# One chunk's transpose moved from TensorE to a DMA that ScalarE gives out

## The chip, the cores and the metric

One core of a Trainium2 chip runs the whole program. The metric is the device time of one launch in microseconds (us). Beside it stands one profiled execution, whose span reaches from its first to its last instruction. Engines: PE is TensorE's matmul side and PEld its weight load, DVE is VectorE, ACT is ScalarE, POOL is GpSimd, SP is SyncE. SP does no arithmetic here; its instructions give out DMAs. ACT can give out DMAs too, on a queue of its own; in the profile such instructions are listed as SPq and ACTq.

## The reference

A retention layer feeds a gated feed-forward layer. Inputs are float32: q, k, v of shape (8 batches, 8 heads, 576 positions, 64) and three weight matrices.

```python
scores = (1 / sqrt(64)) * q @ k.T                     # per batch and head
gamma  = 1 - 2.0 ** (-5 - head)
ret    = (scores * where(i >= j, gamma ** (i - j), 0)) @ v
x      = ret.transpose(0, 2, 1, 3).reshape(4608, 512)
out    = (sigmoid(x @ w_gate) * (x @ w_val)) @ w_out  # w_gate, w_val 512x1536; w_out 1536x512
```

## The kernel before

The 4608 tokens are worked off in chunks of 128 positions. The first 768 tokens go as three pairs of chunks; every later chunk is a *step* `s` (0 to 29), a batch and a chunk of it from the table `STEPS`. The powers of gamma are multiplied into q and k when they are cast to bf16 (`cast_qk`, line 420, into the tile `qk_s`; k's part on POOL, q's part on DVE for steps 0 and 1 and on POOL after that). The mask then needs only zeros and ones, and what earlier chunks contribute comes from a running state, a 64 by 64 matrix for each head.

TensorE's matmul contracts over partitions, so q and k must stand with the head dimension on the partitions. The tile `T_s` holds them turned. There are two ways to it:

- `cross(s)` (line 446) gives out one DMA crossbar transpose on SP's queue, from `qk_s` to `T_s`. It is called by `casts_to` (line 853) between the casts of k and q and the cast of v, for every step not in `TURNED`.
- `turn_step(s)` (line 624), for the steps in `TURNED = (0, 1, 7)`: eight 128x128 transposes on PE into two PSUM banks, which ACT (the first half of `T_s`) and DVE (the second half) copy out.

Tokens run through the feed-forward layer in blocks: tokens 0 to 511 first, then blocks of 256 (512 to 767, called `w = 0`, and 768 to 1023), then blocks of 512. Every engine works its own list of instructions strictly in the order in which the code recorded it; the framework adds the waits. The code around the change runs so:

1. `op_first` (line 1542) makes the output product of the first 512 tokens: 12 weight slices `fc` into four PSUM tiles. The first `FIRST_OP_CUTS = 20` products with `fc > 0` are written as two halves of 256 columns.
2. Between its last slices stands `turn_step(0)`; after it `casts_to(1)` casts step 1.
3. The block `w = 0` runs its hidden units (`h_units`, line 877): for six pairs of slices a gate tile `h_g` (8 matmuls, then a sigmoid on ACT into `gv`) and a value tile `h_v` (8 matmuls, then a multiplication on DVE into `gv`). Both come from the same three PSUM banks, tag `ffn`, dealt round: `h_v_4` takes the bank that `h_g_2` had, and so waits until ACT has read `h_g_2`.
4. Into these units the string `SUMS_AT` deals small jobs. An entry such as `0.6:t01p` means: in block 0, before unit 6, job `t` (`turn_step`) for step 1. `0.0:c03p` is `casts_to(3)`, which casts steps 2 and 3 and gives out their transposes and the loads of step 4 on SP.
5. After unit 10 of `w = 0` the first two steps are used: `slot_of_two` (line 741) makes their scores (`row`, line 686) from `T_0` and `T_1`, and the products of k and v for the state.

DMAs are counted on eight semaphores, DMAHW0 to DMAHW7, that the framework deals round in the order in which DMAs are recorded, whatever queue gives them out; each DMA waits at least for the one that had its semaphore before.

Of the kernel before, what the change touches and what calls it, by code (L numbers as in the profile page):

```python
# [16 lines left out]
def kernel(  # L17
# [19 lines left out]
    nc = tc.nc  # L37
# [109 lines left out]
    def half(x):  # L147
        return slice(x * 64, x * 64 + 64)
# [169 lines left out]
    def wo_sums(i, part, parts, eng=nc.vector):  # L318

        fp = slice(part * (NFC // 2) // parts, (part + 1) * (NFC // 2) // parts)  # L320
        b11, b12, b21, b22 = (wo_sb[:, r::2, c:c + DM // 2][:, fp] for r in range(2) for c in (0, DM // 2))
        t1, t2, t4 = (wt_sb[:, j, fp] for j in range(3))
        to, a, b = ((t1, b12, b11), (t2, b22, t1), (b12, b22, b12), (t4, b21, t2))[i]
        eng.tensor_tensor(out=to, in0=a, in1=b, op=ALU.subtract)
# [34 lines left out]
    def w_sums(kind, i, u, eng):  # L359

        a11, a12, a21, a22 = w_quarters(kind, u)
        s1, s2, s4 = (wt3_sb[kind][j][u] for j in range(3))
        to, a, b, op = ((s1, a21, a22, ALU.add), (s2, s1, a11, ALU.subtract), (seventh(kind, u), a11, a21, ALU.subtract),
                        (s4, a12, s2, ALU.subtract))[i]
        eng.tensor_tensor(out=to, in0=a, in1=b, op=op)
# [54 lines left out]
    def cast_qk(s, i, eng):  # L420
        c = STEPS[s][1]
        if i == 1:
            natural_qk[s] = nat_pool.tile([P, 2, M, P], BF16, tag="qk", name=f"qk_{s}")
        to = natural_qk[s][:, i].rearrange("p m (y d) -> p y m d", y=2)
        if i == 1 and s >= SCALED_V:
            (on_pool if s in K_ON_POOL else on_act)(out=to, in_=by_halves(loaded[s][0]))
            return
        tab = (qtab, ktab)[i][:, c, :].rearrange("p (y m) -> p y m", y=2).unsqueeze(3).to_broadcast([P, 2, M, D])
        eng.tensor_tensor(out=to, in0=by_halves(loaded[s][1 - i]), in1=tab, op=ALU.mult)  # L429
# [8 lines left out]
    def cast_v(s, eng):  # L438
        natural["v", s] = nat_pool.tile([P, H, D], BF16, tag="v", name=f"v_{s}", bufs=6)
        if s >= SCALED_V:  # L440
            tab = ktab[:, STEPS[s][1], :].unsqueeze(2).to_broadcast([P, H, D])
            nc.gpsimd.tensor_tensor(out=natural["v", s], in0=loaded[s][2], in1=tab, op=ALU.mult)  # L442
        else:
            eng(out=natural["v", s], in_=loaded[s][2])

    def cross(s):
        t = att_pool.tile([P, 2, M, P], BF16, tag="T", name=f"T_{s}", bufs=6)
        nc.sync.dma_start_transpose(out=t.rearrange("p j m t -> p (j m) t"),
                                    in_=natural_qk[s].rearrange("p j m d -> p (j m d)"))
        turned[s] = t  # L450

# [167 lines left out]
            cols = slice(t0, t0 + P)  # L619
            eng(out=x_out(slice(i * k, (i + 1) * k), cols), in_=x_in(ps[:, at_m:at_m + k], cols))  # L620

    TURNED = (0, 1, 7)

    def turn_step(s):

        t = att_pool.tile([P, 2, M, P], BF16, tag="T", name=f"T_{s}", bufs=6)
        for i, ((pool, tag), eng) in enumerate(zip(VALS, (on_act, on_dve))):
            ps = pool.tile([P, M, P], BF16, tag=tag, name=f"turn_{s}_{i}")
            for m in range(M):
                nc.tensor.matmul(ps[:, m, :], lhsT=natural_qk[s][:, i, m, :], rhs=ident, is_transpose=True,  # L630
                                 start=(m == 0), stop=(m == M - 1))
            eng(out=t[:, i], in_=ps)
        turned[s] = t
# [6 lines left out]
    def new_state(key, dt=BF16):  # L640
        b, c, j = key
        if dt == BF16 and c == LAST - 1 and j == NJ - 1:
            return nat_pool.tile([P, M, D], dt, tag="sf", name=f"sf_{b}_{c}_{j}", bufs=5)
        tag, bufs = ("s32", 3) if dt == FP32 else ("sb", 4)
        if (tag, b, c) not in both_steps:
            both_steps[tag, b, c] = nat_pool.tile([P, NJ, M, D], dt, tag=tag, name=f"{tag}_{b}_{c}", bufs=bufs)
        return both_steps[tag, b, c][:, j]
# [142 lines left out]
    def after_two(vals, news, i, late, first, closes):  # L790

        if i == 0 and not news:
            for s in vals:
                inter(s, [(1,), (0,)])
        if i < NJ:
            if len(vals) == 2 and at_col[vals[1]] == at_col[vals[0]] + P:
                leave_two(vals, i)
            else:
                for s in vals:
                    nc.scalar.copy(out=x_out(ALL, cols_of(s, i)), in_=x_in(val_ps[s][i], cols_of(s, i)))  # L800
        if i == NJ:
            for s in vals:
                if dealt(cols_of(s, 0)):
                    x_sums(at_col[s], X_LATE if late and closes else X_FIRST)
        if late and news and i == (NJ if closes else NJ - 1):
            casts_to(min(done["cast"], news[-1] + LEAD_CAST + 1) if first and not closes else news[-1] + LEAD_CAST + 1)
        for n, s in enumerate(news):
            b, c = STEPS[s]
            if c == LAST:
                continue  # L810
            if i == n:
                add_state(s, 0)
                add_state(s, 1)
                if s < 2 * len(PAIRS_AT) and s == max(x for x in news if STEPS[x][1] < LAST):
                    ffn_psum.free_last(ffn_psum.held.pop())
            if i == n + 1:
                keep_both(b, c, [j for j in range(NJ) if totals.pop((s, j), None) is not None], on_act)
# [16 lines left out]
    def first_batch_state():  # L834

        whole = new_state((0, LAST - 1, NJ - 1))
        for hh in range(2):
            for y in range(2):
                (nc.vector.tensor_copy if hh == y else nc.sync.dma_start)(
                    out=whole[half(y), hh::2, :], in_=sbd[3][half(hh), 2 * y:2 * y + 2, half(hh)])  # L840
        state[0, LAST - 1, NJ - 1] = whole
# [6 lines left out]
    def loads_to(s):  # L848
        while done["ld"] <= min(NS - 1, s):
            load(done["ld"])  # L850
            done["ld"] += 1

    def casts_to(s):
        while done["cast"] <= min(NS - 1, s):
            x = done["cast"]
            loads_to(x + (AHEAD[x] if x < len(AHEAD) else 2))
            cast_qk(x, 1, nc.gpsimd)
            cast_qk(x, 0, nc.vector if x < 2 else nc.gpsimd)
            if x not in TURNED:
                cross(x)  # L860
            cast_v(x, on_dve if x == 0 else on_act if x in V_ON_ACT else on_pool)
            done["cast"] += 1
# [6 lines left out]
    def next_two(vals, news, late, first, closes):  # L869
        slot_of_two(vals, news)  # L870
        if news and not late:
            casts_to(news[-1] + 2)
        for i in range(3):
            pending.append(lambda i=i: after_two(vals, news, i, late, first, closes))
# [661 lines left out]
    for i in (0, 1, 3):  # L1536
        w_sums("g", i, 1, nc.vector)

    FIRST_OP_CUTS = 20
    op_cut = []  # L1540

    def op_first(fcs, nbs, opps):
        for fc in fcs:
            for nb in nbs:
                parts = 2 if fc and len(op_cut) < FIRST_OP_CUTS else 1
                op_cut.extend([fc] * (parts - 1))
# [27 lines left out]
    keep_state((1, 0, 1), st_tiles[1], on_act)  # L1574
    op_first((5, 6, 7, 8, 9), range(3), opps)
    casts_to(0)
    third_intra([PV, QK[0]])
    pair_st(2, 1)
# [15 lines left out]
    store(opps[3], 3 * P, on_act)  # L1594
    casts_to(1)

    SUMS_AT = ("0.0:c03p 0.1:f00p 0.3:g00p 0.3:w10v 0.3:w11v 0.6:t01p 0.7:o10p 0.8:c02v "
# [4 lines left out]
    sums_at = {}  # L1602
    for x in SUMS_AT:
        at, x = x.split(":")
        u, i, eng = int(x[1]), int(x[2]), nc.gpsimd if x[3] == "p" else nc.vector
        sums_at.setdefault(tuple(int(y) for y in at.split(".")), []).append(
            lambda k=x[0], u=u, i=i, eng=eng: wo_sums(i, u, 3, eng) if k == "o" else
            casts_to(10 * u + i) if k == "c" else turn_step(i) if k == "t" else first_batch_state() if k == "f" else
            w_sums(k, i, u, eng))
    PAIRS_AT = ((0, 10), (0, 11), (1, 10), (1, 0))  # L1610
    paired = 0
# [80 lines left out]
```

## Time and profile before

| what | value |
|---|---|
| median of 3 runs | 304.57 us (303.11 to 306.47) |
| profiled execution, its own time | 303.89 us |
| profiled execution, span | 302.2 us |
| PE busy | 295.6 us, 98% of the span |
| DVE, POOL, ACT busy | 230.4, 225.8, 204.9 us |
| mean granted TensorE clock | 0.999 |
| crossbar transposes | 27, all on SP's queue |

A line of the timeline gives start, length, engine, line of the kernel, operation, output and input, and how many instructions it merges; in square brackets stands the idle time just before and what ended it. The profiled execution is 1.69 us longer than its span, for what lies before the first and after the last instruction.

### The profile page before, as it was taken

How to read it: one execution, taken by the hardware profiler on the slowest of the kernel's cores; microseconds unless marked ns; L12 is line 12 of the kernel's file. 1: busy time of each engine (PE TensorE's matmuls, PEld its weight loads, DVE VectorE, ACT ScalarE, POOL GpSimd, SP SyncE). 2: the span in 40 equal slices, each digit the busy share in tenths (PEclk: the TensorE clock that was granted, in tenths of full speed). 3: DMA queues.
4: the chain of work that ended last, by engine and by line, in shares of the span. 5: the costliest groups of instructions: out<-in, count | busy, mean ns of one | idle time of the engine just before them, and what ended most of it. 6: DMA issues, size and time to landing. Idle time of an engine off the chain costs nothing.

```text
span 302.2 us, 10696 instructions
## 1 busy us (share of the span) xinstructions
PE 295.6 (98%) x4437; PEld 250.0 (83%) x4437; DVE 230.4 (76%) x439; ACT 204.9 (68%) x414; POOL 225.8 (75%) x253
## 2 busy tenths in 40 slices
PE   7999999999999999999999999999999999999994
PEld 3677876978868888888888888888888888888883
DVE  5967895796986998789748974896489848935893
ACT  6755565335369657985798589857985698559830
POOL 5775854846669888978997898789978946860780
PEclk9999999999999999999999999999999999999999
DMA  7999999979998989999749967976694165004013
GB/s 205 336 370 379 322 334 229 210 160 202 213 175 184 257 173 196 219 201 262 141 108 199 259 143 155 218 185 143 124 204 132 37 123 193 4 2 139 3 36 104
DMA packets 146464, 54.99 MB, mean 182 GB/s; under 512 B 124400, under 2 KB 139760, under 8 KB 146416
## 3 DMA queue, kind: packets, MB, share of 16 engines
q1 hardware_dynamic: 145328, 53.59, 73.6%
q8 instruction: 34, 0.56, 0.8%
q10 hardware_dynamic: 1088, 0.72, 0.8%
q14 instruction: 14, 0.11, 0.1%
HBM read 37.75 MB, written 9.44 MB: 156 GB/s over the span
## 4 chain that ended last, share of the span: by engine, by line
PE 92%; DVE 2%; DMA 2%; issue 1%; ACT 1%; POOL 0%; SPq 0%; DVEq 0%
PE gatea L1046 12%; PE wa L1046 11%; PE qa L1173 11%; PE qe L1173 9%; PE gatee L1046 6%; PE we L1046 5%; PE op L1549 4%; PE h_v L886 3%; PE h_g L886 3%; PE gateg L1046 3%; PE wg L1046 3%; PE hv L1374 3%; PE op L1306 3%; PE val L718 2%; PE qa L1249 2%; PE hg L1374 2%
## 5 line engine op out<-in xcount | busy, mean ns | idle before, releaser
L1046 PEld LDWEIGHTS <-wg_sb 128*128 128x128 bf16 x348 | 34.1, 98 | 4.1
L1073 POOL TENSOR_TENSOR gv<-gv,wu 128x512 bf16<-128x512 bf16 x20 | 23.5, 1174 | 15.5 <-DVE wu L1085 15.4
L1173 PEld LDWEIGHTS <-gsum 128*128 128x128 bf16 x312 | 30.0, 98 | 3.7
L429 POOL TENSOR_TENSOR qk<-q,qtab 128x512 bf16<-128x512 f32 x28 | 30.3, 1082 | 3.5 <-DMA q<-in_q_dram 3.5
L1046 PEld LDWEIGHTS <-wv_sb 128*128 128x128 bf16 x296 | 28.9, 98 | 3.6 <-issue 0.2
L1085 DVE TENSOR_TENSOR gu<-gatee,gu 128x512 f32<-128x512 f32 x22 | 15.2, 690 | 19.4 <-ACT gateg L1077 10.2
L943 POOL TENSOR_TENSOR gsum<-gsum,gv 128x256 bf16<-128x256 bf16 (+1 forms) x20 | 17.6, 890 | 14.4 <-DVE gsum L943 12.6
L1046 PEld LDWEIGHTS <-wgt_sb 128*128 128x128 bf16 x264 | 25.8, 98 | 3.0
L1046 PE MATMUL gatea<-xsum,wg_sb 128*128 128x256 bf16 x172 | 25.6, 273 | 0.0
L1173 PEld LDWEIGHTS <-gv 128*128 128x128 bf16 x228 | 21.8, 98 | 2.7
L1088 DVE TENSOR_TENSOR gs<-gatea,gs 128x512 f32<-128x512 f32 x22 | 15.2, 689 | 9.5 <-PE gatea L1046 9.4
L943 POOL TENSOR_TENSOR gsum<-gv,gsum 128x256 bf16<-128x256 bf16 (+1 forms) x24 | 21.9, 922 | 0.2
L429 POOL TENSOR_TENSOR qk<-k,ktab 128x512 bf16<-128x512 f32 x11 | 11.6, 1054 | 13.4 <-DMA k<-in_k_dram 13.2
L704 DVE TENSOR_TENSOR pt<-row,tri 128x512 bf16<-128x512 f32 x30 | 19.2, 680 | 2.8 <-PE row L686 2.6
L442 POOL TENSOR_TENSOR v<-v,ktab 128x512 bf16<-128x512 f32 x19 | 20.9, 1101 | 0.0
L1046 PE MATMUL wa<-xsum,wv_sb 128*128 128x256 bf16 x136 | 20.4, 273 | 0.1
L658 ACT CAST sb<-s 128x512 bf16<-128x512 f32 (+1 forms) x26 | 14.3, 569 | 8.8 <-DVE s L829 8.7
L788 ACT CAST xT<-val 128x512 bf16<-128x512 f32 x26 | 14.7, 592 | 7.0 <-PE val L734 7.0
L943 DVE TENSOR_TENSOR gsum<-gv 128x512 bf16<-128x512 bf16 (+1 forms) x34 | 19.1, 589 | 0.0
L1046 PEld LDWEIGHTS <-wvt 128*128 128x128 bf16 x168 | 16.4, 98 | 1.9
L943 POOL TENSOR_TENSOR gsum<-gv 128x256 bf16<-128x256 bf16 (+1 forms) x20 | 17.6, 882 | 0.0
L1071 ACT ACTIVATE gv<-gs 128x512 bf16<-128x512 f32 x22 | 13.9, 633 | 5.4 <-DVE gs L1088 5.4
(210 smaller groups left out, 883.9 us busy)
## 6 DMA issues: line engine op xcount, KB each, us to landing
k<-in_k_dram SPq DMA_DIRECT2D x26, 256.0 KB, 3.9
q<-in_q_dram SPq DMA_DIRECT2D x26, 256.0 KB, 4.2
v<-in_v_dram SPq DMA_DIRECT2D x26, 256.0 KB, 4.6
out_dram<-ob SPq DMA_DIRECT2D x24, 256.0 KB, 2.7
wg<-in_moe_w_gate_dram SPq DMA_DIRECT2D x12, 256.0 KB, 5.4
wv<-in_moe_w_val_dram SPq DMA_DIRECT2D x12, 256.0 KB, 5.6
wo<-in_moe_w_out_dram SPq DMA_DIRECT2D x12, 256.0 KB, 5.6
v32p<-in_v_dram SPq DMA_DIRECT2D x6, 256.0 KB, 4.5
```

Source lines behind the costliest of these rows:

```text
L429: eng.tensor_tensor(out=to, in0=by_halves(loaded[s][1 - i]), in1=tab, op=ALU.mult)
L442: nc.gpsimd.tensor_tensor(out=natural["v", s], in0=loaded[s][2], in1=tab, op=ALU.mult)
L704: nc.vector.tensor_tensor(out=t[:, y, 0:n].rearrange("p i m t -> p (i m) t"), in0=rows_tile[ss[0]][y][:, 0:n].rearrange("p i m t -> p (i m ...
L788: nc.scalar.copy(out=to, in_=src)
L886: nc.tensor.matmul(ps[:, i], lhsT=w_sb[:, kc, (fc + i) * P:(fc + i + 1) * P], rhs=xT(kc, slice(t0, t0 + n)), start=(kc == 0), stop=(kc == ...
L943: eng.tensor_tensor(out=to, in0=a, in1=b, op=op)
L1046: nc.tensor.matmul(ps[:, f], lhsT=w[:, kc, f * P:(f + 1) * P], rhs=x[:, kc], start=(first and f == 0 and kc == 0), stop=(f == 1 and kc == ...
L1073: eng.tensor_tensor(out=to, in0=to, in1=src[:, part], op=ALU.mult)
L1085: nc.vector.tensor_tensor(out=me["u2"], in0=e, in1=me["u2"], op=ALU.add)
L1088: nc.vector.tensor_tensor(out=me["s5"], in0=a, in1=me["s5"], op=ALU.add)
L1173: nc.tensor.matmul(ps[:, b], lhsT=left(fp)[:, b * P:(b + 1) * P], rhs=right(fp), start=(first and fp == 0 and b == 0), stop=(fp == NFC // ...
L1374: nc.tensor.matmul(ps[:, cols], lhsT=(wg_sb if what == "g" else wv_sb)[:, kc, fc * P:(fc + 1) * P], rhs=xT(kc, cols), start=(kc == 0), sto ...
```

## The change

Step 1 leaves `TURNED` and is turned by `cross`, given out by ACT (`nc.scalar`) in place of SP. The call stands at `0.0:x01p`, in front of unit 0 of `w = 0` and behind `casts_to(3)`; the entry `0.6:t01p` is gone. `FIRST_OP_CUTS` goes from 20 to 28, so eight more products of `op_first` are written as halves: 16 instructions more on PE (a weight load and a matmul each), as many as `turn_step(1)` had.

```diff
-    def cross(s):
+    ON_ACT = (1,)
+
+    def cross(s, queue=nc.sync):
         t = att_pool.tile([P, 2, M, P], BF16, tag="T", name=f"T_{s}", bufs=6)
-        nc.sync.dma_start_transpose(out=t.rearrange("p j m t -> p (j m) t"),
+        queue.dma_start_transpose(out=t.rearrange("p j m t -> p (j m) t"),
                                     in_=natural_qk[s].rearrange("p j m d -> p (j m d)"))
         turned[s] = t
...
-    TURNED = (0, 1, 7)
+    TURNED = (0, 7,)
...
-            if x not in TURNED:
+            if x not in TURNED + ON_ACT:
                 cross(x)
...
-    FIRST_OP_CUTS = 20
+    FIRST_OP_CUTS = 28
...
-    SUMS_AT = ("0.0:c03p 0.1:f00p 0.3:g00p 0.3:w10v 0.3:w11v 0.6:t01p 0.7:o10p 0.8:c02v "
+    SUMS_AT = ("0.0:c03p 0.1:f00p 0.3:g00p 0.3:w10v 0.3:w11v 0.0:x01p 0.7:o10p 0.8:c02v "
...
-            casts_to(10 * u + i) if k == "c" else turn_step(i) if k == "t" else first_batch_state() if k == "f" else
+            casts_to(10 * u + i) if k == "c" else turn_step(i) if k == "t" else cross(i, nc.scalar) if k == "x" else first_batch_state() if k == "f" else
```

The orders below name semaphores with the engine or DMA lane that raises them; a tile's last number is a running one, so `T_1_1203` is `T_1`. ScalarE around the place, before (lines behind 448 have numbers two higher after the change):

```order
L918 COPY ob_384_1151<-op_0_3_1121 128x512 [waits PE_49]
L889 ACTIVATE gv_512_0_1164<-h_g_512_0_1165 128x2x256 [waits PE_49]
L889 ACTIVATE gv_512_0_1164<-h_g_512_2_1210 128x2x256 [waits PE_49]
L889 ACTIVATE gv_512_1_1233<-h_g_512_4_1234 128x2x256 [waits PE_49]
L889 ACTIVATE gv_512_1_1233<-h_g_512_6_1254 128x2x256 [waits PE_49]
L632 COPY T_1_1264<-turn_1_0_1265 128x512 [waits PE_49]
```

The same place of ScalarE after the change:

```order
L920 COPY ob_384_1159<-op_0_3_1129 128x512 [waits PE_49]
L891 ACTIVATE gv_512_0_1172<-h_g_512_0_1173 128x2x256 [waits PE_49]
L450 DMA_TRANSPOSE T_1_1203<-qk_1_1167 128x8x128 [waits DMAHW1_49,DMAHW0_49,DMAHW4_49,DVE_49,Pool_49]
L891 ACTIVATE gv_512_0_1172<-h_g_512_2_1220 128x2x256 [waits PE_49]
L891 ACTIVATE gv_512_1_1243<-h_g_512_4_1244 128x2x256 [waits PE_49]
L891 ACTIVATE gv_512_1_1243<-h_g_512_6_1264 128x2x256 [waits PE_49]
```

The copy of `T_1` behind the sigmoid of `h_g_6` is gone, and the transpose of step 1 stands between the sigmoids of `h_g_0` and `h_g_2`, with waits on three DMA lanes. SP's list at the same place, after the change (`k32`, `q32`, `v32` are loads, `sf` a small copy of a state):

```order
L450 DMA_TRANSPOSE T_2_1186<-qk_2_1183 128x8x128 [waits DMAHW4_49,PE_49,Pool_49]
L171 DMA k32_4_1190<-in_k_dram 128x8x64 [waits DMAHW5_49]
L171 DMA q32_4_1192<-in_q_dram 128x8x64 [waits DMAHW6_49]
L171 DMA v32_4_1194<-in_v_dram 128x8x64 [waits DMAHW7_49,Activation_49]
L450 DMA_TRANSPOSE T_3_1199<-qk_3_1196 128x8x128 [waits DMAHW0_49,PE_49,Pool_49]
L841 DMA sf_0_3_1_1215<-sbd3_265 64x2x64 [waits DMAHW2_49]
L841 DMA sf_0_3_1_1215<-sbd3_265 64x2x64 [waits DMAHW3_49]
L450 DMA_TRANSPOSE T_4_1401<-qk_4_1398 128x8x128 [waits DMAHW1_49,DVE_49,DMAHW4_49,PE_49,Pool_49]
```

Its order is that of before; what is new is in the waits. Lane 0 is that of `T_3`, lane 4 that of `T_2`, and lane 1 is now that of `T_1`, which is recorded between `T_3` and the first `sf`; before, the first `sf` had lane 1, and `T_4` waited for lane 3 alone of the DMA lanes:

```order
L448 DMA_TRANSPOSE T_3_1191<-qk_3_1188 128x8x128 [waits DMAHW0_49,PE_49,Pool_49]
L839 DMA sf_0_3_1_1205<-sbd3_265 64x2x64 [waits DMAHW1_49]
L839 DMA sf_0_3_1_1205<-sbd3_265 64x2x64 [waits DMAHW2_49]
L448 DMA_TRANSPOSE T_4_1404<-qk_4_1401 128x8x128 [waits DVE_49,DMAHW3_49,PE_49,Pool_49]
L171 DMA k32_5_1408<-in_k_dram 128x8x64 [waits DMAHW4_49,Activation_49]
```

So the framework has tied every transpose to the last ones of the other queue: `T_1` on ACT to `T_2` and `T_3` on SP, and `T_4` on SP to `T_1` on ACT. On PE the eight transposes of step 1, which stood between the matmuls of `h_g_6` and `h_v_6`, are gone.

## The prediction

> **What bounds the kernel now.** I read the page first, then who waited for whom, then busy time by stretch, and last the timeline around the change.
>
> ```profile
> PE 295.6 (98%) x4437; PEld 250.0 (83%) x4437; DVE 230.4 (76%) x439; ACT 204.9 (68%) x414; POOL 225.8 (75%) x253
> ...
> PE 92%; DVE 2%; DMA 2%; issue 1%; ACT 1%; POOL 0%; SPq 0%; DVEq 0%
> ```
>
> PE is busy 98% of the span and holds 92% of the chain that ended last. The stretches around the change (first numbers: length, PE busy) say the same with less averaging:
>
> ```profile
> 45.00:60.00 15.00, 15.00 (x172) 11.17 (x170) 10.05 (x18) 6.72 (x14) 8.99 (x10) 1.00 0.97 218
> 60.00:90.00 30.00, 29.93 (x628) 23.37 (x626) 24.19 (x48) 14.11 (x29) 18.43 (x20) 1.00 0.94 192
> ...
> 120.00:150.00 30.00, 30.00 (x501) 26.72 (x499) 25.78 (x49) 23.58 (x48) 27.26 (x28) 1.00 0.94 199
> ...
> 250.00:295.00 45.00, 45.00 (x570) 39.87 (x568) 33.31 (x59) 30.96 (x65) 30.22 (x29) 1.00 0.18 58
> ```
>
> PE stands idle 0.07 us in these 45 us; ACT works 6.72 of 15. So PE time removed here shortens the run one to one, a wait of PE lengthens it one to one, and no later idle time of PE is there to give it back (the four stretches from 120 to 295 us, of which the first and the last are shown, are full to the hundredth). The change takes a little off PE, and it puts a wait on ACT. The question is only whether PE feels it.
>
> **What is removed.** The transposes of step 1, in the chain of PE and in the timeline of ACT and DVE:
>
> ```profile
> 57.62 0.45 PE turn L630 x8
> ...
> 58.15 0.58 ACT L632 COPY T<-turn 128x512 bf16<-128x512 bf16 x1
> 58.23 0.41 DVE L632 COPY T<-turn 128x512 bf16<-128x512 bf16 x1
> ```
>
> On PE this is 0.45 us of the chain: a gain of 0.45. The two copies go too, 0.58 on ACT and 0.41 on DVE, but neither engine bounds the stretch, so they count for nothing.
>
> **What is cut.** Eight products of 512 columns become sixteen of 256.
>
> ```profile
> 39.98 1.97 PE op L1549 x18
> ...
> 50.64 0.86 PE op L1549 x4
> ```
>
> The eighteen halves take 0.109 each, the four whole ones 0.215. Sixteen halves against eight whole: 1.75 less 1.72, a cost of 0.03 us.
>
> **What is added: a transpose on ACT with a wait for SP's transposes.** By the orders above, ACT may not give out `T_1` before `T_2` and `T_3` have landed: it waits for their lanes, DMAHW4 and DMAHW0. These are the instructions of the timeline that matter (SPq rows are the giving out, not the transfer):
>
> ```profile
> 52.41 0.60 ACT L889 ACTIVATE gv<-h_g 128x512 bf16<-128x512 f32 x1 [0.29 <-PE h_g L886]
> ...
> 54.16 0.60 ACT L889 ACTIVATE gv<-h_g 128x512 bf16<-128x512 f32 x1 [1.15 <-PE h_g L886]
> ...
> 55.53 1.70 SPq L448 DMA_TRANSPOSE T<-qk  x1
> 55.60 0.86 PEld L886 LDWEIGHTS <-wv_sb 128*128 128x128 bf16 x8
> 55.70 1.04 PE L886 MATMUL h_v<-xT,wv_sb 128*128 128x256 bf16 x8
> ...
> 57.39 1.22 POOL L429 TENSOR_TENSOR qk<-q,qtab 128x512 bf16<-128x512 f32 x1
> ...
> 58.58 1.29 SPq L171 DMA_DIRECT2D v<-in_v_dram  x1
> ...
> 59.98 1.88 SPq L448 DMA_TRANSPOSE T<-qk  x1
> ...
> 61.48 0.45 PE L686 MATMUL row<-T 64*64 64x64 bf16 x32
> ```
>
> ACT reaches the transpose at 53.0, when the sigmoid of `h_g_0` ends. `T_3` is only given out at 59.98, behind the last cast of step 3 on POOL (to 58.61) and the loads of step 4 (the last to 59.87), and nothing in the change can bring that forward: POOL's and SP's lists are as before. When does it land? For that transpose alone, and for all 27:
>
> ```profile
> L448 SPq DMA_TRANSPOSE T<-qk x1: 1877/1877/1877, 60.0 to 60.0; - x1
> ...
> DMA to landing us min/median/max: 4.2/4.2/4.2
> ...
> L448 SPq DMA_TRANSPOSE T<-qk x27: 1232/1697/4111, 55.5 to 244.0; - x27
> ...
> DMA to landing us min/median/max: 2.7/4.2/6.1
> ```
>
> From its start it took 4.2, so it lands at 59.98 + 4.2 = **64.18**. Until then ACT stands. Is an engine really held by a DMA instruction that waits? On SP it is:
>
> ```profile
> 105.20 0.85 SPq L171 DMA_DIRECT2D v<-in_v_dram  x1
> 108.86 1.23 SPq L448 DMA_TRANSPOSE T<-qk  x1
> 110.13 0.59 SPq L171 DMA_DIRECT2D k<-in_k_dram  x1
> ```
>
> SP gave out nothing from 106.05 to 108.86, and the load behind the transpose came after it. On ACT, the start of the program shows that giving out occupies it:
>
> ```profile
> 1.34 0.52 ACTq L186 DMA_DIRECT2D q32p<-in_q_dram  x1
> ...
> 1.89 1.28 ACT L261 ACT_TABLE_LOAD   x1 [1.89 <-issue]
> ```
>
> The table load starts when the second load has been given out, at 1.86.
>
> How long ACT takes to give out a transpose no row shows. The nearest row is SP's next one, at the same place:
>
> ```profile
> 63.60 1.96 SPq L448 DMA_TRANSPOSE T<-qk  x1
> ```
>
> I take its 1.96; the ends are 1.23 and 4.11, from the 27 above. Two separate waits ahead of it cost a few hundredths; I put 0.06 for them. So ACT is free at 64.18 + 0.06 + 1.96 = 66.20.
>
> What is queued behind it? The sigmoid of `h_g_2`, which ran at 54.16. `h_v_4` needs its bank, so that sigmoid (0.60) must end, at 66.80, before PE can start `h_v_4`; the row at 55.70 is `h_v_4`. From an end on ACT to PE took 0.06 elsewhere (`sb` ends at 65.28 + 1.07 = 66.35, the weight load that waited for it starts at 66.41):
>
> ```profile
> 65.28 1.07 ACT L658 CAST sb<-s 128x512 bf16<-128x512 f32 x2 [3.09 <-DVE s L829]
> ...
> 66.41 0.14 PEld L734 LDWEIGHTS <-sb 64*64 64x64 bf16 x6 [0.18 <-ACT sb L658]
> ```
>
> `h_v_4` starts at 66.86 in place of 55.70: PE loses **11.16 us**. The slack that this has to use up first is small: ACT could have been held until 55.70 - 0.60 - 0.06 = 55.04 for nothing.
>
> What is late next? DVE's product with `h_v_2` waits for the same sigmoid and follows at once; from there the units run as before. `T_1` itself, given out at 64.24, lands by 70.4 even with the longest landing, 6.1. PE comes to the scores (61.48 before) 5.3 us of units after 66.86, at 72.2 or later, so they don't wait. `T_4` on SP waits for `T_1` and goes out about 5 us later than its 63.60, and the loads behind it too, but PE is 11 us late by then: no loss.
>
> **What the idle time does to the clock.** PE would stand for 11 us, which it does nowhere in the middle of this run. The trace has two places that bear on it. At the start, ten equal matmuls behind an idle PE, and three later ones:
>
> ```profile
> 1.05 4.02 PE L242 MATMUL idle<-blank 128*128 128x512 bf16 x10 [1.05 <-DVE blank L229]
> ...
> 5.79 0.81 PE L242 MATMUL idle<-blank 128*128 128x512 bf16 x3
> ```
>
> And the granted clock (third number from the right) by the microsecond:
>
> ```profile
> 1.00:2.00 1.00, 0.95 (x3) 1.00 0.02 7
> ...
> 298.00:299.00 1.00, 0.27 (x3) 0.00 (x0) 0.50 (x2) 0.00 (x0) 0.00 (x0) 1.00 0.84 244
> ...
> 301.00:302.20 1.20, 0.00 (x0) 0.00 (x0) 0.00 (x0) 0.00 (x0) 0.00 (x0) 0.70 0.00 0
> ```
>
> The matmul record is 0.379 long when alone and at full pace, so the three at 5.79 are (0.81 - 0.379) / 2 = 0.216 apart; ten at that pace would take 2.32, and they took 4.02. The slow start cost 1.70. At the end the last matmul ends at 298.27, and the clock falls to a mean of 0.70 in the last 1.2 us: at half, for 0.72 us, so from 301.5, about 3.2 us after PE stopped. But the granted clock reads 1.00 between 1 and 2 us, where matmuls were slow; it does not decide by itself. I count the restart like the start: **1.70 us**, with nothing and twice as much as its ends.
>
> [...]
>
> **The sum.** 11.16 (stall) + 1.70 (restart) + 0.03 (cuts) - 0.45 (transposes) = +12.44 on the profiled execution's 303.89: **316.3 us**. That execution lies 0.7 below the median of the three runs (304.57), inside their spread of 3.4.
>
> **The rivals.** The third one needs the landing of `T_2`, given out at 55.53:
>
> ```profile
> DMA to landing us min/median/max: 3.8/3.8/3.8
> ```
>
> - *No slow restart* (17%). The stall as above, the clock stays: 314.6. For it speaks only the 1.00 at the start.
> - *A slower giving out* (9%). SP once took 4.11 for a transpose under load; with that ACT is held 2.15 longer: 318.5.
> - *Held, but only by `T_2`* (3%). If the wait on lane 0 were met by an earlier DMA of that lane, the release would be the landing of `T_2`, 55.53 + 3.8 = 59.33. With its 1.70 to give out, 0.60 and 0.12 `h_v_4` starts at 61.75, 6.05 late: 303.89 + 6.05 + 1.70 - 0.42 = 311.2. Against it: `T_1` has no data from any other DMA of lane 0.
> - *Not slower* (4%). ACT passes the waiting transpose to its queue and goes on. Then the sigmoid of `h_g_2` runs at 54.8 at the latest (53.0 + 1.7 to give out, less than the 55.04 at which PE would feel it), and what is left is -0.45 + 0.03: 303.5. It decides if ACT is free before 55.04. Against it: the idle 2.8 us of SP ahead of 108.86.
>
> [...]
>
> **How the numbers follow.** The central case holds 67%, and 96% lies well above the time before. The range leaves out `T_2`, the case of no wait, and the longest giving out together with a slow restart twice as long. Its low end is no slow restart with the shortest giving out (314.6 - 0.73 = 313.9), less 0.9 for the spread of runs; its high end the slow giving out with 0.5 for the same: 313.0 to 319.0. A change within 1% (3 us) is about what a measurement of this kernel cannot tell from none: 4% for that, 1% for faster, 95% for slower.
>
> **What would show it.** In the changed profile: ACT without an instruction from 53 to past 64, an ACTq transpose near 64.2 of 1.2 to 2 us, PE idle from about 56 to 67 and again full from there, its first dozen matmuls after that about 0.21 apart for 256 columns in place of 0.11, the granted clock below 1 in slices 8 to 9 of 40, and `T_4` on SP near 68. `h_v_4` starting before 60, or the first scores waiting for `T_1`, would make the argument wrong.

## The result, and the profile after

The changed kernel took 316.49 us (median of 4 runs, 316.36 to 316.86) against 304.23 (4 runs, 303.11 to 306.47): a ratio of 1.042 [1.038, 1.046], 12.3 us slower. The profiled execution took 316.42 and its span is 314.6, 12.4 more than before. The forecast was 316.3, within 313.0 to 319.0.

Busy times, clock and queues from the page of the changed kernel. q8 is the queue that fetches instructions (packets, MB, share):

```profile
PE 296.2 (94%) x4431; PEld 250.9 (80%) x4437; DVE 231.0 (73%) x438; ACT 204.5 (65%) x413; POOL 225.0 (72%) x253
...
PEclk9999999759999999999999999999999999999999
...
q8 instruction: 34, 0.56, 0.7%
```

PE does as much work as before (296.2 us for 295.6) in a span 12.4 longer, so it stood idle; and the granted clock falls below 1 in two slices, at 55 to 71 us. Who waited for whom, first PE over the whole run, then ACT in the stretch from 50 to 80 us:

```profile
PE h_v L888 <- ACT gv L891: 11.0, 1, 11.0
...
PE h_g L888 <- DVE gv L893: 0.8, 1, 0.8
```

```profile
ACT gv L891 <- issue: 13.2, 1, 13.2
```

One wait of PE holds 11.0 of the 12.4 us: `h_v_4` for a sigmoid on ACT. ACT itself shows 13.2 us of "issue", which is a wait for nothing that its own rows name; the row of the semaphore names it. On ACT's queue, between 59.5 and 61 us:

```profile
L450 ACTq EVENT_SEMAPHORE  x1: 8043/8043/8043, 56.6 to 56.6; - x1
```

This is a pure wait: 8.04 us from 56.6, until 64.65. The chain that ended last says what ended it, step by step (its first row here belongs to the wait before that one):

```profile
52.50 4.11 DMA k<-in_k_dram
...
60.39 4.26 DMA T<-qk
64.65 0.03 ACTq L450
...
64.79 1.34 ACTq L450
66.12 0.05 issue
66.17 0.61 ACT gv L891
66.78 0.04 issue
66.82 1.86 PE h_v L888 x8
68.68 1.34 PE h_g L888 x8
70.03 0.87 PE h_v L888 x8
```

`T_3`, given out by SP at 60.39, lands at 64.65; two waits on semaphores end within 0.14; ACT gives out `T_1` in 1.34; the sigmoid of `h_g_2` runs; `h_v_4` starts. Its eight matmuls take 1.86, the next eight 1.34, and only the third eight run at the pace of before, 0.87.

ACT stood before 56.6 too, from the end of its sigmoid at 52.93, and this part is the wait for lane 1. The trace gives the same semaphore to `T_1` and to the load of k for step 3, which was given out at 52.50 and landed at 56.61. So ACT had two long waits one behind the other, one for the DMA that had used its lane before and one for `T_3`; the second ended last and set the stall.

### The profile page after: what moved, and what is told of

Same layout as the page of the kernel before. It is cut to its first block, busy times and chain, and to the rows that moved or that the text cites. A ratio compares the mean times of both kernels' runs of the same rounds, so it can differ in the third digit from the quotient of the medians.

```text
span 314.6 us, 10689 instructions
## 1 busy us (share of the span) xinstructions
PE 296.2 (94%) x4431; PEld 250.9 (80%) x4437; DVE 231.0 (73%) x438; ACT 204.5 (65%) x413; POOL 225.0 (72%) x253
## 4 chain that ended last, share of the span: by engine, by line
PE 81%; DMA 9%; SPq 3%; DVE 3%; POOL 2%; issue 1%; ACTq 0%; ACT 0%; DVEq 0%; POOLq 0%
PE gatea L1048 12%; PE wa L1048 11%; PE qa L1175 10%; PE qe L1175 9%; PE gatee L1048 6%; PE we L1048 6%; DMA k<-in_k_dram 4%; PE op L1308 3%; PE gateg L1048 3%; PE wg L1048 3%; PE h_v L888 3%; SPq L186 3%; PE h_g L888 2%; DMA wv<-in_moe_w_val_dram 2%; PE val L720 2%; DMA v<-in_v_dram 2%
## 5 line engine op out<-in xcount | busy, mean ns | idle before, releaser
L1048 PEld LDWEIGHTS <-wg_sb 128*128 128x128 bf16 x348 | 34.0, 98 | 4.2
L1048 PEld LDWEIGHTS <-wv_sb 128*128 128x128 bf16 x296 | 29.0, 98 | 3.4
L1048 PEld LDWEIGHTS <-wgt_sb 128*128 128x128 bf16 x264 | 25.8, 98 | 3.0
L1048 PE MATMUL gatea<-xsum,wg_sb 128*128 128x256 bf16 x172 | 25.7, 273 | 0.0
L888 PE MATMUL h_v<-xT,wv_sb 128*128 128x256 bf16 x96 | 13.3, 284 | 11.0 <-ACT gv L891 11.0
L891 ACT ACTIVATE gv<-h_g 128x512 bf16<-128x512 f32 x12 | 7.1, 597 | 25.2 <-issue 13.2
L893 DVE TENSOR_TENSOR gv<-gv,h_v 128x512 bf16<-128x512 bf16 x12 | 8.2, 686 | 18.3 <-ACT gv L891 11.3
L1048 PE MATMUL wa<-xsum,wv_sb 128*128 128x256 bf16 x136 | 20.4, 273 | 0.0
L888 PEld LDWEIGHTS <-wv_sb 128*128 128x128 bf16 x96 | 9.5, 101 | 12.6 <-issue 11.2
```

Source lines behind the costliest of these rows:

```text
L888: nc.tensor.matmul(ps[:, i], lhsT=w_sb[:, kc, (fc + i) * P:(fc + i + 1) * P], rhs=xT(kc, slice(t0, t0 + n)), start=(kc == 0), stop=(kc == ...
L1048: nc.tensor.matmul(ps[:, f], lhsT=w[:, kc, f * P:(f + 1) * P], rhs=x[:, kc], start=(first and f == 0 and kc == 0), stop=(f == 1 and kc == ...
```

## The experiments

A short `...` in the diffs stands for the rest of the string `SUMS_AT`. All are against the changed kernel except `e4`, which is against the one before. The kernel before ran beside each of them, with a median of 303.2 beside e1 to e4 and 303.6 beside the others, so times from different experiments are best compared by what they lie above it (12.3 for the changed kernel above its own 304.23).

### Where the transpose is recorded: e1, e2, e6

First theory: what stalls PE is not that ACT gives out a transpose, but which transposes of SP are recorded ahead of it. If so, moving one entry of the string moves the stall.

**e1_first** puts it ahead of both:

```diff
-"0.0:c03p 0.1:f00p 0.3:g00p 0.3:w10v 0.3:w11v 0.0:x01p ..."
+"0.0:x01p 0.0:c03p 0.1:f00p 0.3:g00p 0.3:w10v 0.3:w11v ..."
```

> The changed kernel with its two jobs in front of unit 0 swapped: T_1 on ScalarE is recorded ahead of casts_to(3), so it waits for no transpose of SP, and T_2 on SP waits for T_1. Theory (ScalarE is held by the landing of T_3): ScalarE gives out T_1 at about 53 and is free at 54.3 to 55, PE waits at h_v_4 for 0 to 0.4 us, the clock stays up, and the run comes to about 303.5 to 304 on the profiled execution's 303.9 of before. Rival (a transpose given out by ScalarE is slow in itself, or two queues disturb each other): still several us slower, 306 or more.

Measured: 304.82 (10 runs), ratio 1.006 [1.003, 1.008]. From its timeline:

```profile
51.93 1.04 PE L888 MATMUL h_g<-xT,wg_sb 128*128 128x256 bf16 x8
...
53.09 1.34 ACTq L450 DMA_TRANSPOSE T<-qk  x1
...
58.33 1.35 SPq L450 DMA_TRANSPOSE T<-qk  x1
...
61.63 0.45 PE L688 MATMUL row<-T 64*64 64x64 bf16 x32
62.08 2.34 SPq L450 DMA_TRANSPOSE T<-qk  x1
...
67.27 0.32 PE L688 MATMUL row<-T 64*64 64x64 bf16 x16 [0.47 <-DMA T<-qk]
```

ACT gives out the same transpose at 53.09 and the stall is gone. The wait has not gone, it has changed sides: now SP holds `T_2` until 58.33 (55.53 before) and `T_3` until 62.08, and the scores of step 3 wait 0.47 for it. The run is still 1.6 slower than the kernel before beside it, between its expectation and the rival. Part of this lies ahead of the change: the first unit of `w = 0` starts 0.59 later than before, behind a wait of 0.66 for POOL at 22.8 us, and what caused that wait was not followed. The row at 51.93 is that first unit; from there to the first scores are 9.70 us, against 10.14 before (51.34 to 61.48): the removal of PE's transposes is worth 0.44.

**e2_between** records `T_1` between the two:

```diff
-"0.0:c03p 0.1:f00p 0.3:g00p 0.3:w10v 0.3:w11v 0.0:x01p ..."
+"0.0:c02p 0.0:x01p 0.0:c03p 0.1:f00p 0.3:g00p 0.3:w10v 0.3:w11v ..."
```

> The changed kernel with T_1 recorded between T_2 and T_3, so that ScalarE waits for the landing of T_2 alone. Theory: release at 55.8 + 4.1 = 59.9, 1.34 to give out, 0.6 for the sigmoid; h_v_4 starts at 62.1 in place of 66.8, PE waits 6.4 us in place of 11.0, the restart costs its 1.3 again, and the run comes to about 311.5. Rival (the wait is not that for the last transpose recorded on SP): 316.4 as before, or 304.

Measured: 311.4 (one run). Timeline:

```profile
59.66 1.33 ACTq L450 DMA_TRANSPOSE T<-qk  x1
...
61.69 1.86 PE L888 MATMUL h_v<-xT,wv_sb 128*128 128x256 bf16 x8 [5.68 <-ACT gv L891]
```

PE waits 5.7 us in place of 11.0. So the stall is set by the last transpose of SP that is recorded ahead of ACT's: none, `T_2`, or `T_3` give 0, 5.7, and 11.0. (The move also gives `T_1` another lane. In e1 that lane was free when ACT came to it at 53.0; in the changed kernel the lane alone would have held ACT until 56.6.)

**e6_later** leaves `T_1` behind `T_3` and moves it to where `turn_step(1)` stood, behind the sigmoids of the units before unit 6:

```diff
-"0.0:c03p 0.1:f00p 0.3:g00p 0.3:w10v 0.3:w11v 0.0:x01p ..."
+"0.0:c03p 0.1:f00p 0.3:g00p 0.3:w10v 0.3:w11v 0.6:x01p ..."
```

> The changed kernel with the call of cross at the place of the old turn_step(1), behind h_g_6, so that ScalarE is held from about 58.3 and not from 53. T_3 is still what it waits for. Theory: the release stays near 64.7 and T_1 lands near 67.6, but PE goes on with h_v_6, h_g_8, h_v_8 and h_g_10 and only stops at the scores (61.0): it waits 6.5 us there, for the landing and not for ScalarE; with 1.3 for the restart and 0.45 off, 311.2. Rival (what counts is how long ScalarE is held): PE loses 6.5 us and the sigmoids behind it besides, 313 or more.

Measured: 308.87 (one run). Timeline:

```profile
61.28 0.32 PE L688 MATMUL row<-T 64*64 64x64 bf16 x16
62.42 1.33 ACTq L450 DMA_TRANSPOSE T<-qk  x1
...
65.32 0.43 PE L688 MATMUL row<-T 64*64 64x64 bf16 x16 [3.73 <-DMA T<-qk]
```

The sigmoids run ahead of the wait, PE reaches the scores of step 0 at 61.28, and then it waits for the data of `T_1` itself. The 2.3 us by which the run beat its expectation are the release: ACT gave out at 62.42, while the expectation had put this where the changed kernel had it, near 64.7. When `T_3` is given out differs by run, from 57.98 here to 60.39 in the changed kernel. The moved place cuts the stall, but not to nothing: PE takes its list in order, and the next instructions of the list are the scores that need `T_1`.

### The same transpose on SP: e5, e9, e10

The rival theory: `T_1` by the crossbar is too late wherever it is given out. **e5_on_sp** gives it out on SP, in `casts_to(1)`:

```diff
-    ON_ACT = (1,)
+    ON_ACT = ()
```

(and the entry `0.0:x01p` is dropped).

> The changed kernel with T_1 given out by SP in place of ScalarE, in casts_to(1), ahead of T_2. Theory (the loss is the wait between two queues, the transposes on PE cost 0.44 us): ScalarE is never held, no stall at h_v_4, scores of steps 0 and 1 come 0.45 us sooner than before. SP has 1.7 us more to give out ahead of T_2 and T_3, so T_3 lands at about 66 to 67 and the scores of steps 2 and 3 may wait up to 0.8 us: 303 to 304 where the kernel before has 303.2 on that chip. Rival (any DMA transpose in place of PE's is bad here): 305 or more.

Measured: 304.28 (10 runs), ratio 1.002 [1.000, 1.004]. Timeline of SP, and the one new wait of PE:

```profile
54.06 3.61 SPq L450 DMA_TRANSPOSE T<-qk  x2
```

```profile
PE wa L1048 <- DVE ws L1090: 0.6, 1, 0.6
```

`T_1` and `T_2` go out together from 54.06, in 3.61 us with no wait between the two, and from the first unit of `w = 0` (51.51) to the scores (61.21) it is again 9.70 us in place of 10.14. The scores start 0.27 earlier than before, and at 103.1 us a wait of 0.6 for DVE takes that back. By the interval the crossbar alone costs 0.4% at most; what costs 4% in the changed kernel is the second queue with its order of recording.

**e9_sp_loads_behind** and **e10_first_loads_behind** try to make something of e5 and e1: the loads of step 4, which SP gives out between `T_2` and `T_3`, move behind the transposes, so that `T_3` goes earlier.

```diff
-    AHEAD = (2, 2, 1, 1, 0, 1, 1, 0, 1, 2, 1, 1)
+    AHEAD = (2, 2, 1, 0, 0, 1, 1, 0, 1, 2, 1, 1)
```

> As the run with T_1 on SP, and the loads of step 4 given out behind T_3 in place of ahead of it (AHEAD[3] from 1 to 0). Theory: T_1, T_2 and T_3 follow one another on SP from 54, T_3 lands near 62, no score waits, ScalarE is not held, PE gets its 0.45 us; the loads of step 4 come some 4 us later, when POOL needs them at 61, so POOL's casts of step 4 are at 66 to 68 and T_4 at 69, needed at 80: 303.1 where the kernel before has 303.6, a gain of 0.45 that five rounds may just show. Rival (DVE and POOL, not PE, set the pace in the first block of 512, and take back what PE gains): no difference or up to 0.3 slower.

> As the run with T_1 recorded first on ScalarE, and the loads of step 4 behind T_3. Theory: ScalarE gives out T_1 at 53 without waiting and is free at 54.4; T_2 waits for T_1 (58.2), T_3 goes out right behind it at 59.7 and lands at 64 to 65, so the scores of steps 2 and 3 (66) do not wait, which cost the first such run 0.5 to 0.8 us: 303.1 to 303.6 on a chip where the kernel before has 303.6, 0.5 to 1 us faster than with the loads ahead of T_3. Rival (the loss of that run lay elsewhere): 1 us slower than before again.

Measured: 306.24 (7 runs), ratio 1.008 [1.005, 1.011], and 306.31 (6 runs), ratio 1.008 [1.006, 1.010]. The waits of PE, first of e9, then of e10:

```profile
PE wa L1048 <- DVE ws L1090: 1.3, 1, 1.3
...
PE row L688 <- DMA T<-qk: 0.8, 1, 0.8
```

```profile
PE row L688 <- DMA T<-qk: 2.0, 2, 1.7
```

e10 has the same wait of 1.3 for DVE at L1048. Both are some 2.7 slower than the kernel before, which neither the theory nor the rival of either had. The loads that were put back bring the next transpose late: SP gives out `T_4` at 67.25 (e9) and 68.21 (e10), in e5 at 63.64, and later scores wait for such a transpose (in e10 those at 80.45 wait 1.7). Why DVE is late at L1048 was not followed. No kernel tried here beats the one before.

### What the pause costs in clock: e3, e7

Second theory: of the 12.3 us, over one is not waiting but a slow restart. If PE is given needless matmuls during the pause, which write zeros that nothing reads, the restart cost has to go and the stall stays.

**e3_busy**:

```diff
+    def keep_busy(n):
+        t = tr_psum.tile([P, 4, P], FP32, tag="tr", name="busy")
+        for _ in range(n):
+            nc.tensor.matmul(t, lhsT=blank, rhs=blank.unsqueeze(1).to_broadcast([P, 4, P]), start=True, stop=True)
...
-"... 0.0:x01p 0.7:o10p ..."
+"... 0.0:x01p 0.4:z00p 0.7:o10p ..."
```

where the job `z` calls `keep_busy(46)`.

> The changed kernel with 46 needless matmuls of 512 columns (on zeros, into a free PSUM bank, read by nobody) in front of h_v_4, which keep PE busy for some 9.9 of its 11.0 us of waiting. Theory (the 1.3 us after the wait are the clock that fell for want of work): the granted clock stays at 1.00, h_v_4's eight matmuls take 1.04 in place of 1.86, and the run comes to 315.1. Rival (the slow restart has another cause, such as weights or tiles that come late): 316.4.

Measured: 317.78 (2 runs), ratio 1.048 [1.046, 1.050]: a miss, slower instead of faster (14.6 above the kernel before on its chip, where the changed kernel is 12.3 above). The timeline and the waits of PE:

```profile
55.49 10.09 PE L1607 MATMUL busy<-blank 128*128 128x512 bf16 x46
65.42 1.04 PE L888 MATMUL h_v<-xT,wv_sb 128*128 128x256 bf16 x8
...
70.75 0.45 PE L688 MATMUL row<-T 64*64 64x64 bf16 x32
```

```profile
PE val L736 <- issue: 1.6, 1, 1.6
...
PE qa L1175 <- issue: 0.9, 1, 0.9
PE qe L1175 <- issue: 0.5, 1, 0.5
```

The restart did what was expected: `h_v_4` takes 1.04 in place of 1.86, and from its start to the scores are 5.33 us. The run lost elsewhere, in 3.0 us of "issue" of PE, a wait that no other engine ends. These waits were not there in the changed kernel. In the two profiled runs the account nearly closes: `h_v_4` starts 1.40 earlier, the restart saves 1.30, "issue" costs 3.04, a wait of PE for DVE is 0.34 longer, which makes +0.68 where +1.20 was measured; 0.52 stays open. What had changed on PE is the number of instructions: 92 more (a weight load and a matmul each), and one packet more on q8 (35 for 34).

**e7_busy_256** tests that reading with the same length of needless work in 256 instructions more, a whole packet by the count (PE has 8874 matmuls and weight loads before, and if the 34 packets of q8 are PE's, they come to some 261 each; at the 16384 bytes that each has in the trace of before, that is an estimated 63 bytes for an instruction, which the expectation takes as 64):

```diff
+    def keep_busy(wide, narrow):
+        t = tr_psum.tile([P, 4, P], FP32, tag="tr", name="busy")
+        for j in range(wide + narrow):
+            k = 2 if j < wide else 1
+            nc.tensor.matmul(t[:, 0:k], lhsT=blank, rhs=blank.unsqueeze(1).to_broadcast([P, k, P]), start=True, stop=True)
```

called with 36 and 92.

> The changed kernel with 128 needless matmuls (36 of 256 columns and 92 of 128, on zeros) in front of h_v_4: some 9.1 us of work for PE in its 11 us of waiting, and 256 instructions more on PE, where the first such run had 92. Theory: the clock stays up, the restart's 1.3 us are saved, and since the number of instructions is a multiple of 256, which is what one instruction packet of 16 KB holds if an instruction has 64 bytes, PE does not meet the waits of 0.5 to 1.6 us without a releaser that the run with 92 had: 315.1. Rival (those waits come from the needless work itself, not from where the instructions stand): about 317.8 again.

Measured: 313.95 (2 runs), ratio 1.032 [1.028, 1.037], 10.4 above the kernel before. Timeline and packets:

```profile
55.41 9.23 PE L1608 MATMUL busy<-blank 128*128 128x256 bf16 x128
...
63.15 1.34 ACTq L450 DMA_TRANSPOSE T<-qk  x1
...
65.18 1.03 PE L888 MATMUL h_v<-xT,wv_sb 128*128 128x256 bf16 x8 [0.54 <-ACT gv L891]
...
70.51 0.45 PE L688 MATMUL row<-T 64*64 64x64 bf16 x32
```

```profile
q8 instruction: 35, 0.57, 0.8%
```

No "issue" wait of PE is left behind `h_v_4`, and again 5.33 us lie between it and the scores. In the changed kernel that stretch took 6.63 (66.82 to 73.45). The restart costs 6.63 - 5.33 = **1.30 us**. The profiled run is 3.06 below the changed kernel's: 1.64 because `h_v_4` could start earlier (65.18 for 66.82), 1.30 for the restart, 0.12 open.

### The cuts: e4, e8

**e4_cuts** is the kernel before with the cuts alone, **e8_no_cuts** the changed one without them:

```diff
-    FIRST_OP_CUTS = 20
+    FIRST_OP_CUTS = 28
```

```diff
-    FIRST_OP_CUTS = 28
+    FIRST_OP_CUTS = 20
```

> The kernel before with FIRST_OP_CUTS at 28, nothing else: the cuts alone. Theory: 0.03 us of PE, so no difference that can be measured, 304.2. Rival (more weight loads or other places of the instructions cost something): 1 us or more.

> The changed kernel with FIRST_OP_CUTS back at 20: without the cuts PE has 16 instructions fewer from the place of the old transposes on. Theory (the cuts serve to keep the places of the later instructions, which decide whether PE waits for its own instructions): one or more waits of PE without a releaser, 0.3 to 2 us in sum, 316.8 to 318.5. Rival (the cuts do nothing): 316.4 to 316.6.

Measured: e4 304.35 (6 runs), ratio 1.004 [1.002, 1.006], 1.1 slower than the kernel before beside it, as the rival had it, with less than half of that in the wait below and the rest open; e8 314.57 (2 runs, 313.25 and 315.89), ratio 1.034 [1.028, 1.041]. A wait of PE from e4, then three rows of e8 (two waits, and ACT's giving out in the timeline):

```profile
PE qe L1173 <- issue: 0.5, 1, 0.5
```

```profile
PE h_v L888 <- ACT gv L891: 8.6, 1, 8.6
...
PE val L736 <- issue: 0.7, 1, 0.7
```

```profile
62.80 1.34 ACTq L450 DMA_TRANSPOSE T<-qk  x1
```

Sixteen instructions more on PE (e4) or sixteen fewer (e8) bring an "issue" wait of 0.5 or 0.7 that neither kernel has when both halves of the change are made.

The traces put it down to the fetch. Take PE's list with all its records in order. The waits of e4, e8 and e3 stand behind record 3521 (e4, at 117.1 us), 7105 (e8, at 242.6) and 4289, 5313 and 5569 (e3, at 152.8, 185.5 and 188.4): each is 193 plus a multiple of 256. In the traces of before and of the changed kernel all 34 packets of q8 have 16384 bytes, 64 for each of 256 instructions, and behind each of the 33 such places PE goes on after the k-th packet has landed, 1.25 us later or more (before) and 1.26 or more (changed). At the one wait of this kind before, at 16.96 us behind record 449, it is the 1.25. So a change in the number of instructions moves these places to other work: in e3 PE went through the 256 from 186.00 on in 2.4 us and then stood for 1.6.

e8's time doesn't answer its expectation: `T_3` landed 2 us earlier in the profiled run, and its two runs lie 2.6 apart. In that profiled run `h_v_4` starts 1.99 earlier than in the changed kernel, the restart is 0.63 longer (7.26 from `h_v_4` to the scores, for 6.63) and the "issue" wait is 0.69: together 0.67 faster, with 0.53 measured. What the missing cuts cost over more runs stays open.

## Why the prediction was right

The mechanism is the one that it gave: ACT is held by its own transpose until SP's `T_3` has landed, and the sigmoid behind it holds PE. e1 and e2 take that wait away in whole and in half, and the stall follows. One wait was left out: the order after the change lists lane 1 among the waits of `T_1`, and the prediction went by lanes 0 and 4 alone. Lane 1 held ACT until 56.61, past the 55.04 up to which a hold is free. It was covered by the longer wait, so the sum is not touched. But without the wait for SP's transposes `h_v_4` would have started at an estimated 58.8 (56.61, then 0.14, 1.34 and 0.70 by the rows of the chain), 3.1 us late: the change would have cost time even so. The terms of the sum, of which some are off in both directions:

- **When `T_3` lands**: forecast 64.18, measured 64.65. The landing was right (4.26 for 4.2); the giving out was 0.41 later, at 60.39. Over the runs that keep `T_1` behind `T_3`, the giving out moves by 2.4 us (57.98 to 60.39), more than any other term: a single profile of before gave it to no better than that.
- **The waits on ACT**: 0.14 for 0.06.
- **Giving out on ACT**: mis-sized. Taken from SP's next transpose as 1.96, it measured 1.34, and 1.33 or 1.34 in every kernel in which ACT gave it out. The choice of the nearest row in place was wrong, and the shorter end of the range (1.23) was the better guess. SP's queue is busy and ACT's was empty; that this makes the difference was not tested.
- **The start of `h_v_4`**: 66.82 for 66.86. The three errors above cancel (0.47 and 0.08 late, 0.62 early). This term is right partly by luck.
- **The restart**: 1.30 (e7) for 1.70. Windows of the changed kernel (the third number from the right is the granted clock):

```profile
59.00:60.00 1.00, 0.00 (x0) 0.00 (x0) 0.00 (x0) 0.00 (x0) 1.00 (x2) 0.64 0.63 142
60.00:61.00 1.00, 0.00 (x0) 0.00 (x0) 0.00 (x0) 0.00 (x0) 1.00 (x2) 0.50 1.21 273
...
68.00:69.00 1.00, 1.00 (x7) 0.68 (x5) 0.49 (x2) 0.00 (x0) 0.00 (x0) 0.50 0.01 4
69.00:70.00 1.00, 1.00 (x9) 0.76 (x8) 0.48 (x1) 0.00 (x0) 0.00 (x0) 0.74 1.14 258
```

  In the microseconds before and after these it reads 1.00. A mean of 0.64 is a full clock for 0.28 of that microsecond, so it fell to half at 59.28; 0.74 puts the return at 69.52, 2.7 us after the restart at 66.82. Half of 2.7 is 1.35, near the 1.30. The rival of no slow restart (17%) is out. The one sign for it, the 1.00 between 1 and 2 us, was no reading: the trace of before has no clock record ahead of 4.51 us, and a window without a record reads 1.00.
- **The transposes of PE**: -0.44 (e1) for -0.45.
- **The cuts**: 0.03 is the work that they add by the prediction's rows, and the wrong question. What they do is keep PE's instruction count: apart, each half of the change shows an "issue" wait of 0.5 or 0.7.
- **What was not foreseen**. The scores stand 11.97 us later than before at the first slot, and the span ends 12.4 later. In between, PE's next block waits 0.82 for DVE, which it did not before. Two of the rows in the changed kernel, then the same work before:

```profile
88.08 1.22 POOL L429 TENSOR_TENSOR qk<-k,ktab 128x512 bf16<-128x512 f32 x1
88.32 2.44 DVE L365 TENSOR_TENSOR wg_sb<-wg_sb 128x512 bf16<-128x512 bf16 x2
...
91.41 1.03 PE L888 MATMUL h_g<-xT,wg_sb 128*128 128x256 bf16 x8 [0.82 <-DVE gv L893]
```

```profile
76.38 1.16 DVE L365 TENSOR_TENSOR wg_sb<-wg_sb 128x512 bf16<-128x512 bf16 x2
...
79.20 1.04 POOL L429 TENSOR_TENSOR qk<-k,ktab 128x512 bf16<-128x512 f32 x1 [2.27 <-DMA k<-in_k_dram]
```

  The shift brings POOL's cast over DVE's two sums, which take 2.44 in place of 1.16; before, POOL ended a shorter cast at 76.93 and then waited for a load. e2 (0.7), e3 (1.2), e7 (0.8) and e8 (0.7), the other runs whose `h_v_4` starts late, show the same wait; e1, e5 and e6 do not. Whether the overlap is what makes them longer was not tested. By the rows of the scores the delay is 11.62 at the slot ahead of this wait, 12.74 at the one behind it, and 12.46 at the last slot; the 0.35 that the second slot gave back and this wait are what the sum did not have. With the restart 0.40 below its forecast and this wait above it, the total of 316.3 against 316.42 is closer than its terms: that too is partly luck.

The foretold signs came, but for PE full from there on (the 0.82 above): `T_1` near 64.2 (64.79), `T_4` near 68 (67.76), PE idle from 56 to 67, the clock low in slices 8 and 9. `T_1` landed 2.8 after its giving out, 5.9 ahead of the scores, as the forecast had it.

The wait of a transpose of one queue for the other's is there in each order of recording, at ACT in the changed kernel (until 64.65) and at SP in e1 (until 58.33), and PE waits 11.0, 5.7 or 0 us at `h_v_4` by the order alone. No kernel here with both queues leaves the wait out.

## What to carry to other kernels

A DMA that an engine gives out stands in that engine's own list with all its waits (ACT stood 8.04 us on one of them here), so before moving one to a compute engine, look up which DMAs it must wait for (the one that had its semaphore before among them), when the last of them lands, and what stands behind it: the latest of these sets the stall, not the length of the giving out. If the wait is inevitable, the order of recording chooses which queue bears it (ACT in the changed kernel, SP in e1); put it on the queue that has nothing urgent behind it, or leave all transposes on one queue. And an idle gap on PE of 5.7 to 11 us cost its own length here and then another 1.3 to 1.9 us at half clock. Look at the number of PE's instructions too: 92 or 16 more and 16 fewer brought "issue" waits of 0.5 to 3.0 us here, 256 more none behind the change.

## What the runs showed of the hardware

**The clock after a pause.** Four kernels have a pause of PE after which the clock fell. In the changed kernel PE's last matmul ended at 55.79, and the clock fell at 59.28, 3.5 us later; it came back 2.7 us after the restart. In e2 the windows are these:

```profile
58.00:59.00 1.00, 0.00 (x0) 0.00 (x0) 0.00 (x0) 0.00 (x0) 0.77 (x2) 0.56 0.78 152
...
64.00:65.00 1.00, 1.00 (x6) 0.72 (x5) 0.47 (x1) 0.00 (x0) 0.61 (x1) 0.53 0.00 0
```

They are read like those of the changed kernel: 0.56 puts the fall at 58.12, and 0.53 the return at 64.94. In e8 the windows from 58 and from 68 us read 0.79 and 0.59, in e6 those from 65 and from 68 us read 0.52 and 0.77. All times are us; the restart is what the units up to the scores took above 5.33.

| kernel | PE stopped | clock fell | PE went on | clock back | low for | restart cost |
|---|---|---|---|---|---|---|
| changed | 55.79 | 59.28 (3.5 later) | 66.82 | 69.52 (2.7 later) | 10.24 | 1.30 |
| e8 | 56.27 | 58.58 (2.3 later) | 64.83 | 68.82 (4.0 later) | 10.24 | 1.93 |
| e2 | 56.01 | 58.12 (2.1 later) | 61.69 | 64.94 (3.25 later) | 6.82 | 1.57 |
| e6 | 61.60 | 65.04 (3.4 later) | 65.32 | 68.46 (3.1 later) | 3.42 | not taken |

The two delays differ from run to run, 2.1 to 3.5 us for the fall and 2.7 to 4.0 for the return, but the clock was low for three, three, two and one times 3.41 us. Two stretches at full clock have the same measure: in the changed kernel the one from the first clock record of the trace, 4.66, to the fall at 59.28 is 16 times 3.413, and before the one from 4.51 to the fall at 301.47, behind PE's last matmul, is 87 times 3.413. What decides after which of these multiples the clock falls or comes back, the runs do not show.

**Instruction counts.** PE's list differed by +92, +16, -16, +256 and 0 instructions in e3, e4, e8, e7 and the changed kernel; the "issue" waits that appeared behind the change were 3.0, 0.5, 0.7, 0 and 0 us, all at 193 plus a multiple of 256 records. The kernel before has such a wait too, of 0.28 at 16.96 us, behind record 449. In e3 the 92 instructions cost 3.0 us of such waits where the clock that stayed up saved 1.30, and the place where a changed count cost lay some 70 us (e4) to nearly 200 us (e8) behind the change.
